# z and y in one product of 384 columns, and the gated share added from the same slot: a fused attention and adapter kernel on one core

## The chip, the cores and the metric

The kernel runs on one core of a Trainium2 chip. The core has five engines with queues of their own: TensorE (PE, matmuls, with weight loads shown apart as PEld), VectorE (DVE), ScalarE (ACT), GpSimd (POOL) and SyncE (SP), and 16 DMA engines. Engines wait for each other through semaphores, and each works through its own instructions in order. The metric is the device time of one execution in microseconds (us), the median of several runs.

## The reference

```
qn, kn = q, k divided by their norms over the 6400 tokens
a = softmax(kn^T @ qn / tau)              # 256 x 256 for each of 4 batches
x = v @ a                                 # 25600 tokens x 256
logits = x @ w_gate                       # 8 experts; the best two are kept
w = softmax over the two kept
out = x + sum over the two: w_e * (x @ A_e) @ B_e     # A_e 256x16, B_e 16x256
```

The kernel never forms x to take the logits and the adapters' inner products: with wa = a @ [w_gate, A] (256 x 136) it has logits = v @ wa[:, 0:8] and z = v @ wa[:, 8:136]; then gz = z times the gate of its expert, and out = y + gz @ B with y = v @ a, B being all eight B_e as 128 x 256.

## The kernel before, in words

A chunk is 128 tokens; two chunks are a pair, and there are 100 pairs, 25 for each of four batches. For a batch, q and k are read first. `square` (ACT, or DVE in batch 0) squares them, `gram` (L294) sums k^T q over the 50 chunks in PSUM, and `norm` (L305 for batch 0, L311 for the others) sums the squares. `chain0` to `chain6` then turn the sums into a and wa for the batch.

A pair goes through these steps:

- `transposes` (PE, L444) turns the pair's v so that tokens can be the stationary operand; ACT (L452) or DVE (L454) copies it to SBUF as vT.
- `logits` (PE, L465), for five pairs together, and `gating`, thirteen small operations for five pairs, all but one on DVE (L489 to L534), that give the gates.
- `z_gz`: z on PE (L551, four matmuls of 128 columns), then DVE multiplies by the gates, gz (L555).
- `gz_t`: PE transposes gz (L575) into a spare part of z's bank; DVE (L581), and ACT at the end (L579), copies it out, gzT.
- `y_mm`: y on PE (L567, four matmuls of 256 columns).
- `delta`: PE adds gzT @ B onto y (L587); ACT copies the sum to the output ring `ys` (L591). Full groups leave by DMA from ACT's queue (`send`, L617), the last ones from SP's (L595).

The order is written by hand: the main loop (L678 on) goes through numbered slots, and each engine gets its instructions in the order in which the loop issues them. Slots 8 to 22, 26 to 46 and 50 to 68 also take two to four chunks of `gram` and `norm` for the next batch; the chain's steps lie in the seven slots after each of these stretches. From slot 73 on there is no gram left: this is the tail. Transposes run eight slots ahead of the pair that is gated. Where five further pairs are ready, the loop puts in an iteration of pair work alone, without transposes, gram or a new slot (`behind`); there are six of these.

In a slot the order on PE is: z of pair u; transposes of gz of the pair before, u-1 (`zq`); the first half of the slot's gram; y of the pair u-2 (`dq`); transposes of v for a later pair; the share of u-2; logits every fifth slot; the other half of the gram. A pair so takes three slots. DVE's gating operations are dealt out at a slot's end, up to a sum of estimated costs (`deal`). PSUM has eight banks: one each for gram sums and norm sums, two each for transposed v, z and y; in the tail z also uses the banks of the sums.

Loads are issued by POOL, in a fixed order, as soon as the buffer that they need is free (`load_more`); q, k and v are cast to bf16 on the way.

Of the kernel before, what the change touches and what calls it, by code (L numbers as in the profile page):

```python
# [16 lines left out]
def kernel(  # L17
# [16 lines left out]
    nc = tc.nc  # L34
# [38 lines left out]
    sq_pool = ctx.enter_context(tc.tile_pool(name="sqp", bufs=4))  # L73
    vt_pool = ctx.enter_context(tc.tile_pool(name="vtp", bufs=14))
    y_pool = ctx.enter_context(tc.tile_pool(name="yp", bufs=1))
# [3 lines left out]
    work = ctx.enter_context(tc.tile_pool(name="work", bufs=3))  # L79
    ps_acc = ctx.enter_context(tc.tile_pool(name="psacc", bufs=1, space=bass.MemoryType.PSUM))  # L80
    ps_nrm = ctx.enter_context(tc.tile_pool(name="psnrm", bufs=1, space=bass.MemoryType.PSUM))
    ps_t = ctx.enter_context(tc.tile_pool(name="pst", bufs=2, space=bass.MemoryType.PSUM))
    ps_z = ctx.enter_context(tc.tile_pool(name="psz", bufs=2, space=bass.MemoryType.PSUM))
    ps_y = ctx.enter_context(tc.tile_pool(name="psy", bufs=2, space=bass.MemoryType.PSUM))

# [139 lines left out]

    wg_sb = const.tile([P, CC, E], BF16)
    A_sb = const.tile([P, CC, E, R], BF16)
    ball_sb = const.tile([P, C], BF16)
# [24 lines left out]
    def spread():  # L253

        ap = ps_t.tile([P, 512], FP32, tag="pt", name="A_ps")[:, 0:CC * ER].rearrange(
            "p (c d) -> p c d", c=CC)
        for cc in range(CC):
            for j in range(DL // CC):
                nc.tensor.matmul(ap[:, cc, :], sel[:, E - j:E - j + P], rows[:, j * CC + cc, :],
                                 start=(cc == 0 and j == 0),  # L260
                                 stop=(cc == CC - 1 and j == DL // CC - 1), skip_group_check=True)
        nc.scalar.copy(A_sb.rearrange("p cc e r -> p cc (e r)"), ap)

    def cast_constants():
        nc.vector.tensor_copy(wg_sb.rearrange("p cc e -> p (cc e)"), wst)
        nc.vector.tensor_copy(ball_sb, bst)
# [21 lines left out]
    def gram(b, c):  # L288
        if c == 0:
            acc[b] = ps_acc.tile([P, CC, C], FP32, tag="acc", name="acc")  # L290
        s, o = qk_piece(c)
        t = tiles["qk"][b, s]
        for ic in range(CC):
            nc.tensor.matmul(  # L294
                acc[b][:, ic, :], t[:, 1, o, ic * P:(ic + 1) * P], t[:, 0, o, :],
                start=(c == 0 and ic == 0), stop=(c == NC - 1), skip_group_check=True)
        used("qk", b, c, 1)

    def norm(b, c):
        if c == 0:  # L300
            nrm[b] = ps_nrm.tile([P, 512], FP32, tag="nrm", name="nrm")
        sq = sqs[b, c - c % 2]
        if b == 0:

            nc.tensor.matmul(nrm[b].rearrange("p (w d) -> p w d", w=2), ones_bf, sq[:, :, c % 2, :],  # L305
                             start=(c == 0), stop=(c == NC - 1))
# [52 lines left out]
    def chain3(b):  # L359
        d = st[b]  # L360
        ae = bat.tile([P, CC, C], BF16, name="ae")
# [4 lines left out]
        d["ae"], d["se"] = ae, se  # L366

# [17 lines left out]
    def chain5(b):  # L385
# [4 lines left out]
        for ic in range(CC):  # L390
            for cc in range(CC):
                nc.tensor.matmul(wa[:, ic, 0:E], aT[:, cc, ic * P:(ic + 1) * P], wg_sb[:, cc, :],
                                 start=(cc == 0 and ic == 0), stop=False, skip_group_check=True)
                nc.tensor.matmul(wa[:, ic, E:E + ER], aT[:, cc, ic * P:(ic + 1) * P],
                                 A_sb[:, cc, :, :].rearrange("p e r -> p (e r)"),
                                 start=False, stop=(cc == CC - 1 and ic == CC - 1),
                                 skip_group_check=True)
        wa_sb = bat.tile([P, CC, E + ER], BF16, name="wa_sb")
        for ic in range(CC):
            nc.vector.tensor_scalar(out=wa_sb[:, ic, :], in0=wa[:, ic, :],  # L400
                                    scalar1=rec[:, ic:ic + 1], scalar2=None, op0=OP.mult)
        d["wa"] = wa_sb

    def chain6(b):
        d = st[b]
        a_bf = d["ae"]
        for ic in range(CC):
            nc.vector.tensor_scalar(out=a_bf[:, ic, :], in0=a_bf[:, ic, :],
                                    scalar1=d["rec"][:, ic:ic + 1], scalar2=None, op0=OP.mult)
        d["a"] = a_bf  # L410

# [18 lines left out]
    LAST = {NPT - 9: 4, NPT - 6: 6, NPT - 4: 4, NPT - 3: 2, NPT - 2: 2, NPT - 1: 2}  # L430

    def transposes(g, eng):

# [4 lines left out]
        vt = tiles["v"][b, s]  # L438
        full = ps_t.tile([P, 512], FP32, tag="pt", name="vT_ps")
        pt = full[:, 0:256].bitcast(BF16).rearrange("p (c t) -> p c t", c=CC)  # L440
# [17 lines left out]
    def logits(gr):  # L458
# [4 lines left out]
        for sc in range(n):  # L463
            for ic in range(CC):
                nc.tensor.matmul(lp[:, sc, :], pr[gr["f"] + sc // 2]["vT"][:, ic, sc % 2, :],  # L465
                                 st[b]["wa"][:, ic, 0:E],
                                 start=(sc == 0 and ic == 0), stop=(sc == n - 1 and ic == 1),
# [72 lines left out]

    def z_gz(u):
        b = u // NPAIR
        r, gr = pr[u], groups[u]

        banks = [(ps_z, "zg"), (ps_z, "zg"), (ps_acc, "acc"), (ps_nrm, "nrm")]
        pool, tag = banks[u % 4 if free_banks[0] else 0]
        zg = pool.tile([P, 512], FP32, tag=tag, name="zg")
        z = zg[:, 0:256].rearrange("p (s d) -> p s d", s=2)
        for sc in range(2):
            for ic in range(CC):  # L550
                nc.tensor.matmul(z[:, sc, :], r["vT"][:, ic, sc, :], st[b]["wa"][:, ic, E:E + ER],  # L551
                                 start=(sc == 0 and ic == 0), stop=(sc == 1 and ic == 1),
                                 skip_group_check=True)
        gz = work.tile([P, 2, ER], BF16, tag="gz", name="gz")
        nc.vector.tensor_tensor(  # L555
            out=gz.rearrange("p c (e r) -> p c e r", e=E),
            in0=z.rearrange("p c (e r) -> p c e r", e=E),
            in1=gr["gate"][:, r["w"]:r["w"] + 2, :].to_broadcast([P, 2, E, R]), op=OP.mult)
        r["gz"], r["zg"] = gz, zg

    def y_mm(u):
        b = u // NPAIR
        r = pr[u]
        y = ps_y.tile([P, 2, C], FP32, tag="y", name="y_ps")
        for sc in range(2):
            for ic in range(CC):
                nc.tensor.matmul(y[:, sc, :], r["vT"][:, ic, sc, :], st[b]["a"][:, ic, :],  # L567
                                 start=(sc == 0 and ic == 0), stop=False, skip_group_check=True)
        r["y"] = y
# [14 lines left out]
    def delta(u):  # L584
        r, gr = pr.pop(u), groups[u]
        for sc in range(2):
            nc.tensor.matmul(r["y"][:, sc, :], r["gzT"][:, sc, :], ball_sb, start=False,  # L587
                             stop=(sc == 1), skip_group_check=True)
        if "ys" not in gr:
            gr["ys"] = ring_ys[:, gr["at"], :, :]  # L590
        nc.scalar.copy(gr["ys"][:, r["w"]:r["w"] + 2, :], r["y"])  # L591
        if u in LAST:
# [50 lines left out]
    for f, _ in CHAIN:  # L643
        for g, eng in between.get(f, []):
            transposes(g, eng)
        f(0)
# [31 lines left out]
    while nz < NPT or zq is not None or dq is not None:  # L678
# [14 lines left out]
        if nz < min(slot, NPT) and groups[nz]["ready"]:  # L693
            u = nz
            nz += 1
            z_gz(u)
        if zq is not None:
            gz_t(zq, "act" if slot >= NPT else "dve")
        gram_part(items[:h])
        if dq is not None:  # L700
            y_mm(dq)
        if slot < NPT and not behind:
            transposes(slot, "dve" if items or f is chain3 else "act")
        if dq is not None:
            delta(dq)
        dq, zq = zq, u
        send(max(0, DEFER - max(0, slot - FLUSH) // 3))
# [54 lines left out]
```

## Time and profile before

| | |
|---|---|
| median of 3 runs | 254.23 us (254.2 to 254.32) |
| the profiled execution | 254.42 us, its span 252.6 us |
| PE busy | 219.8 us, 87% |
| weight loads (PEld) | 191.7 us, 76% |
| DVE busy | 154.6 us, 61% |
| ACT busy | 177.5 us, 70% |
| granted PE clock, mean | 0.97 |
| HBM | 78.91 MB read, 26.21 MB written |

The profile is one execution. A row of a timeline has start, length, engine, line, operation, what it writes and reads, and how often; in brackets, the idle time of its engine before it and what ended that. A PE record is longer than the time for which it holds PE, since matmuls are pipelined; the distance between starts gives the latter. A row of stretches has the busy time of each engine in a stretch, the granted clock, the DMA engines' share and what they moved. A row of groups has a line's instructions together: busy time, mean ns of one, idle time before it and what ended it.

### The profile page before, as it was taken

The page shows a single profiled execution, that of the slowest core. Times are in us where ns is not written, and L with a number is a line of the kernel's source. Part 1 is how long each engine was busy: PE and PEld are TensorE (multiplying, and loading weights), DVE is VectorE, ACT ScalarE, POOL GpSimd, SP SyncE. Part 2 cuts the span into 40 slices and gives each one's busy share as a digit, 9 for nine tenths or more (in the row PEclk, how much of TensorE's full clock was granted, in tenths as well). Part 3 has the DMA queues.
Part 4 walks back from the last instruction along what each step waited for, and adds up shares of the span by engine and source line. Part 5 has one row for each costly group of instructions (what it writes and reads, how often), then busy time and mean ns, then how long its engine had stood idle before and what let it go on. Part 6 is the DMA issues. An engine that isn't in the chain of part 4 may idle for free.

```text
span 252.6 us, 7407 instructions
## 1 busy us (share of the span) xinstructions
PE 219.8 (87%) x3122; PEld 191.7 (76%) x3122; DVE 154.6 (61%) x581; ACT 177.5 (70%) x297; POOL 29.8 (12%) x60
## 2 busy tenths in 40 slices
PE   0478877786999999999999999999899799999990
PEld 0235554566899999889999889889798688999970
DVE  1216524655447577776776877858477677776750
ACT  2415532674698979978788798788687677887881
POOL 8210110102012101240220100000001000000000
PEclk9999999659799999999999999999999999999998
DMA  7999999999999999999999999999999999999996
GB/s 213 221 223 214 219 217 211 217 212 218 216 216 213 215 216 213 211 216 213 211 217 220 212 259 270 258 276 296 246 246 353 346 308 413 423 431 417 406 417 259
DMA packets 10577, 66.80 MB, mean 264 GB/s; under 512 B 1584, under 2 KB 1840, under 8 KB 7984
## 3 DMA queue, kind: packets, MB, share of 16 engines
q0 software_dynamic: 7088, 38.80, 74.4%
q10 hardware_dynamic: 1872, 23.59, 22.3%
q1 hardware_dynamic: 1584, 3.94, 4.3%
q8 instruction: 24, 0.39, 0.6%
q14 instruction: 9, 0.07, 0.1%
HBM read 78.91 MB, written 26.21 MB: 416 GB/s over the span
## 4 chain that ended last, share of the span: by engine, by line
PE 51%; DMA 37%; DVE 5%; ACT 3%; POOL 1%; issue 1%; DVEq 0%; POOLq 0%
DMA qk<-in_k_dram 37%; PE y_ps L567 14%; PE acc L294 8%; PE y_ps L587 6%; PE zg L551 6%; PE vT_ps L444 6%; PE zg L575 4%; PE nrm L311 3%; PE vT_ps L465 3%; DVE gz L555 1%; ACT sq L284 1%; ACT ys L591 1%; POOL qk L183 1%; DVE e L497 0%; DVE lg L489 0%
## 5 line engine op out<-in xcount | busy, mean ns | idle before, releaser
L284 ACT ACTIVATE sq<-qk 128x1024 bf16<-128x1024 bf16 (+1 forms) x90 | 89.7, 1026 | 22.6 <-DMA qk<-in_k_dram 16.9
L294 PE MATMUL acc<-qk 128*128 128x256 bf16 x400 | 73.5, 285 | 18.5 <-DMA qk<-in_k_dram 12.1
L591 ACT COPY ys<-y_ps 128x512 f32<-128x512 f32 x100 | 58.7, 588 | 20.7 <-PE y_ps L587 18.7
L567 PE MATMUL y_ps<-ae,vT 128*128 128x256 bf16 x400 | 60.5, 274 | 0.3 <-ACT ys L591 0.3
L294 PEld LDWEIGHTS <-qk 128*128 128x128 bf16 x400 | 34.0, 101 | 28.2 <-DMA qk<-in_k_dram 14.0
L555 DVE TENSOR_TENSOR gz<-zg,gate 128x256 bf16<-128x256 f32 x100 | 41.6, 416 | 14.8 <-PE zg L551 13.0
L311 PEld LDWEIGHTS <-sq 128*128 128x128 bf16 x600 | 36.3, 97 | 6.3 <-ACT sq L284 2.5
L454 DVE COPY vT<-vT_ps 128x512 bf16<-128x512 bf16 x60 | 25.3, 422 | 24.5 <-PE vT_ps L444 23.3
L551 PE MATMUL zg<-wa_sb,vT 128*128 128x128 bf16 x400 | 38.7, 220 | 0.8 <-DVE gzT L581 0.8
L587 PE MATMUL y_ps<-ball_sb,gzT 128*128 128x256 bf16 x200 | 38.6, 275 | 0.0
L311 PE MATMUL nrm<-ones_bf,sq 128*128 128x1 bf16 x600 | 35.6, 164 | 1.3 <-ACT sq L284 1.2
L567 PEld LDWEIGHTS <-vT 128*128 128x128 bf16 x400 | 33.6, 97 | 3.2 <-issue 0.4
L452 ACT COPY vT<-vT_ps 128x512 bf16<-128x512 bf16 x40 | 23.5, 587 | 12.1 <-PE vT_ps L444 10.7
L444 PE MATMUL vT_ps<-ident,vt 128*128 128x128 bf16 x300 | 30.1, 226 | 1.8 <-DVE vT L454 1.5
L575 PE MATMUL zg<-ident,gz 128*128 128x128 bf16 x200 | 27.7, 221 | 1.5 <-DVE gz L555 1.1
L551 PEld LDWEIGHTS <-vT 128*128 128x128 bf16 x400 | 26.3, 97 | 2.7 <-issue 1.3
L444 PEld LDWEIGHTS <-vt 128*128 128x128 bf16 x300 | 23.3, 101 | 4.6 <-issue 2.2
L581 DVE COPY gzT<-zg 128x256 bf16<-128x256 bf16 x90 | 25.1, 279 | 0.0
L286 DVE TENSOR_TENSOR sq<-qk 128x1024 bf16<-128x1024 bf16 (+1 forms) x14 | 9.1, 653 | 21.9 <-DMA qk<-in_k_dram 13.1
L575 PEld LDWEIGHTS <-gz 128*128 128x128 bf16 x200 | 15.1, 98 | 3.1 <-DVE gz L555 2.9
L183 POOL DMA_DIRECT2D qk<-in_q_dram x16 | 8.8, 550 | 69.4 <-PE acc L294 27.6
L587 PEld LDWEIGHTS <-gzT 128*128 128x128 bf16 x200 | 16.3, 99 | 0.5
(77 smaller groups left out, 197.8 us busy)
## 6 DMA issues: line engine op xcount, KB each, us to landing
out_dram<-ys ACTq DMA_DIRECT2D x7, 1280.0 KB, 11.9
out_dram<-ys ACTq DMA_DIRECT2D x2, 3840.0 KB, 24.6
qk<-in_q_dram POOLq DMA_DIRECT2D x8, 768.0 KB, 26.5
qk<-in_k_dram POOLq DMA_DIRECT2D x8, 768.0 KB, 30.0
qk<-in_q_dram POOLq DMA_DIRECT2D x7, 832.0 KB, 24.4
qk<-in_k_dram POOLq DMA_DIRECT2D x7, 832.0 KB, 27.9
out_dram<-ys ACTq DMA_DIRECT2D x2, 2560.0 KB, 20.4
vt<-in_v_dram POOLq DMA_DIRECT2D x4, 1024.0 KB, 34.9
```

The source lines that it names most:

```text
L284: nc.scalar.activation(dst, src, ACT.Square)
L294: nc.tensor.matmul(acc[b][:, ic, :], t[:, 1, o, ic * P:(ic + 1) * P], t[:, 0, o, :], start=(c == 0 and ic == 0), stop=(c == NC - 1), skip_ ...
L311: nc.tensor.matmul(nrm[b][:, j:j + 1], sq[:, w, c % 2, ic * P:(ic + 1) * P], ones_bf[:, 0:1], start=(c == 0 and j == 0), stop=(c == NC - 1 ...
L444: nc.tensor.matmul(pt[:, ic, sc * P:(sc + 1) * P], vt[:, o + sc, ic * P:(ic + 1) * P], ident, is_transpose=True, start=(i == 0), stop=(i = ...
L454: nc.vector.tensor_copy(dst, src)
L551: nc.tensor.matmul(z[:, sc, :], r["vT"][:, ic, sc, :], st[b]["wa"][:, ic, E:E + ER], start=(sc == 0 and ic == 0), stop=(sc == 1 and ic == ...
L555: nc.vector.tensor_tensor(out=gz.rearrange("p c (e r) -> p c e r", e=E), in0=z.rearrange("p c (e r) -> p c e r", e=E), in1=gr["gate"][:, r ...
L567: nc.tensor.matmul(y[:, sc, :], r["vT"][:, ic, sc, :], st[b]["a"][:, ic, :], start=(sc == 0 and ic == 0), stop=False, skip_group_check=True)
L575: nc.tensor.matmul(gt[:, sc, :], r["gz"][:, sc, :], ident, is_transpose=True, start=(sc == 0), stop=(sc == 1))
L581: nc.vector.tensor_copy(gzT, gt)
L587: nc.tensor.matmul(r["y"][:, sc, :], r["gzT"][:, sc, :], ball_sb, start=False, stop=(sc == 1), skip_group_check=True)
L591: nc.scalar.copy(gr["ys"][:, r["w"]:r["w"] + 2, :], r["y"])
```

## The change

z and y of a pair have the same stationary operand, vT. The scaled a and wa now lie beside each other in one tile `ya`, so that one matmul of 384 columns gives z and y of a chunk. A pair's product takes two banks, a chunk in each; two pairs are in PSUM (in the tail three, the third in the banks of the sums, which are now one tile of two banks). The gated z is transposed into the last quarter of a bank of transposed v, that of the slot before where there is one. The slot's order is new. Outside the tail: share of the pair before; product; first half of the gram; transposes of gz of the same pair; transposes of v; logits; second half of the gram (without a gram, v's transposes come before gz's). In the tail: share of pair u-2, transposes of gz of pair u-1, transposes of v, product of pair u, logits. w_gate and A lie in one tile as well (`ga_sb`), so that `chain5` has one matmul where it had two. vT has 12 buffers where it had 14.

```
+    ga_sb = const.tile([P, CC, E + ER], BF16)
...
+            both = ps_sum.tile([P, 2, 512], FP32, tag="sum", name="acc")
+            acc[b] = both[:, 0, :].rearrange("p (c d) -> p c d", c=CC)
+            nrm[b] = both[:, 1, :]
...
+        ya = bat.tile([P, CC, E + ER + C], BF16, name="ya")
+        ae = ya[:, :, E + ER:]
...
+    def bank():
+
+        if pts[0] is None:
+            pts[0] = ps_t.tile([P, 512], FP32, tag="pt", name="vT_ps")
+        return pts[0]
...
-    def z_gz(u):
+    def yz_gz(u):
...
+        if free_banks[0] and u % 3 == 0:
+            t = ps_sum.tile([P, 2, 512], FP32, tag="sum", name="yz")
+        else:
+            t = ps_yz.tile([P, 2, 512], FP32, tag="yz", name="yz")
         for sc in range(2):
             for ic in range(CC):
+                nc.tensor.matmul(t[:, sc, 0:ER + C], r["vT"][:, ic, sc, :], st[b]["ya"][:, ic, E:],
+                                 start=(ic == 0), stop=False, skip_group_check=True)
...
-        gt = r["zg"][:, 256:384].bitcast(BF16).rearrange("p (s d) -> p s d", s=2)
+        gt = (bank() if pts[1] is None else pts[1])[:, 512 - ER:].bitcast(BF16).rearrange("p (s d) -> p s d", s=2)
...
+        pts[:] = [None, pts[0]]
         load_more()
+        if dq is not None:
+            delta(dq)
...
-            z_gz(u)
-        if zq is not None:
-            gz_t(zq, "act" if slot >= NPT else "dve")
-        gram_part(items[:h])
-        if dq is not None:
-            y_mm(dq)
-        if slot < NPT and not behind:
-            transposes(slot, "dve" if items or f is chain3 else "act")
-        if dq is not None:
-            delta(dq)
-        dq, zq = zq, u
+        if free_banks[0]:
+            if zq is not None:
+                gz_t(zq, "act" if slot >= NPT else "dve")
+            if slot < NPT and not behind:
+                transposes(slot, "act")
+            if u is not None:
+                yz_gz(u)
+            dq, zq = zq, u
+        else:
+            if u is not None:
+                yz_gz(u)
+            gram_part(items[:h])
+            if u is not None and items:
+                gz_t(u, "dve")
+            if not behind:
+                transposes(slot, "dve" if items or f is chain3 else "act")
+            if u is not None and not items:
+                gz_t(u, "dve")
+            dq = u
```

More of the change, by code (lines that the diff above doesn't have):

```diff
@@ L438, in transposes @@
         vt = tiles["v"][b, s]
-        full = ps_t.tile([P, 512], FP32, tag="pt", name="vT_ps")
+        full = bank()
         pt = full[:, 0:256].bitcast(BF16).rearrange("p (c t) -> p c t", c=CC)
@@ L556, in z_gz @@
             out=gz.rearrange("p c (e r) -> p c e r", e=E),
-            in0=z.rearrange("p c (e r) -> p c e r", e=E),
+            in0=t[:, :, 0:ER].rearrange("p c (e r) -> p c e r", e=E),
             in1=gr["gate"][:, r["w"]:r["w"] + 2, :].to_broadcast([P, 2, E, R]), op=OP.mult)
[L559 to L569, printed above, removed]
+        r["gz"], r["yz"] = gz, t
     def gz_t(u, eng):
         r = pr[u]
-        gt = r["zg"][:, 256:384].bitcast(BF16).rearrange("p (s d) -> p s d", s=2)
+        gt = (bank() if pts[1] is None else pts[1])[:, 512 - ER:].bitcast(BF16).rearrange("p (s d) -> p s d", s=2)
         for sc in range(2):
@@ L585, in delta @@
         r, gr = pr.pop(u), groups[u]
+        y = r["yz"][:, :, ER:ER + C]
         for sc in range(2):
-            nc.tensor.matmul(r["y"][:, sc, :], r["gzT"][:, sc, :], ball_sb, start=False,
-                             stop=(sc == 1), skip_group_check=True)
+            nc.tensor.matmul(y[:, sc, :], r["gzT"][:, sc, :], ball_sb, start=False,
+                             stop=True, skip_group_check=True)
         if "ys" not in gr:
             gr["ys"] = ring_ys[:, gr["at"], :, :]
-        nc.scalar.copy(gr["ys"][:, r["w"]:r["w"] + 2, :], r["y"])
+        nc.scalar.copy(gr["ys"][:, r["w"]:r["w"] + 2, :], y)
         if u in LAST:
```

43 lines of the change are left out of this document (12 added, 31 removed).

## The prediction

> **What bounds the kernel now.** I read the page's busy table, its DMA slices and the chain that ended last, then the stretches, to see in which stage that chain lies.
>
> ```profile
> span 252.6 us, 7407 instructions
> ...
> PE 219.8 (87%) x3122; PEld 191.7 (76%) x3122; DVE 154.6 (61%) x581; ACT 177.5 (70%) x297; POOL 29.8 (12%) x60
> ...
> DMA  7999999999999999999999999999999999999996
> ...
> PE 51%; DMA 37%; DVE 5%; ACT 3%; POOL 1%; issue 1%; DVEq 0%; POOLq 0%
> ```
>
> ```profile
> 62.00:80.00 18.00, 18.00 (x268) 16.34 (x266) 10.13 (x37) 14.10 (x21) 2.65 (x5) 0.91 1.04 216
> ...
> 120.00:142.00 22.00, 22.00 (x369) 20.66 (x367) 16.14 (x62) 17.67 (x28) 3.67 (x7) 1.00 1.05 215
> 142.00:160.00 18.00, 17.81 (x287) 16.06 (x285) 13.85 (x55) 16.74 (x29) 1.63 (x4) 1.00 1.04 251
> 160.00:179.00 19.00, 17.69 (x279) 16.12 (x278) 12.62 (x47) 14.32 (x22) 0.00 (x0) 1.00 1.03 282
> ...
> 190.00:200.00 10.00, 8.80 (x137) 7.80 (x135) 7.08 (x31) 7.75 (x19) 0.72 (x2) 1.00 1.01 356
> ...
> 249.00:253.00 4.00, 0.00 (x0) 0.00 (x0) 0.00 (x0) 0.00 (x0) 0.00 (x0) 0.76 0.35 136
> ```
>
> Columns: stretch, its length, busy time of PE, PE's weight loads, DVE, ACT and POOL, then granted clock, DMA share, GB/s. Two resources are full at once. The DMA engines work through the span; only the last stretch has slack, 65% of its 3.6 us, some 2 us. PE idles for long only before 62 us; afterwards it is nearly gapless, 1.31 us short in the 160 to 179 stretch, 1.2 us in 190 to 200. So the kernel cannot get more than about 2 us faster, and anything that makes PE wait after 62 us goes into the end.
>
> **What PE pays per pair.** One tail slot, on PE, in order; the distance from one start to the next is what the instruction holds PE for (its own record is longer by the pipeline's drain):
>
> ```profile
> 221.00 0.39 PE L551 MATMUL zg<-wa_sb,vT 128*128 128x128 bf16 x4
> 221.22 0.28 PE L575 MATMUL zg<-ident,gz 128*128 128x128 bf16 x2
> 221.33 0.60 PE L567 MATMUL y_ps<-ae,vT 128*128 128x256 bf16 x4
> 221.77 0.39 PE L444 MATMUL vT_ps<-ident,qk 128*128 128x128 bf16 x4
> 221.99 0.38 PE L587 MATMUL y_ps<-ball_sb,gzT 128*128 128x256 bf16 x2
> 222.21 0.65 PE L465 MATMUL vT_ps<-wa_sb,vT 128*128 128x8 bf16 x20
> 222.71 0.38 PE L551 MATMUL zg<-wa_sb,vT 128*128 128x128 bf16 x4
> ```
>
> z 0.22, transposes of gated z 0.11, y 0.44, transposes of v 0.22, share 0.22: 1.21 us a pair, and 0.50 for the logits every five pairs. A matmul of 128 columns holds PE 55 ns, one of 256 columns 110 ns. Wider ones, from the start of the kernel:
>
> ```profile
> 20.28 0.60 PE L305 MATMUL nrm<-sq,ones_bf 128*128 128x512 bf16 x2
> 20.71 0.60 PE L294 MATMUL acc<-qk 128*128 128x256 bf16 x4
> ```
>
> 0.43 us for two of 512 columns, 215 ns each. The price is columns, with nothing fixed beside it.
>
> ```profile
> L284 ACT ACTIVATE sq<-qk 128x1024 bf16<-128x1024 bf16 (+1 forms) x90 | 89.7, 1026 | 22.6 <-DMA qk<-in_k_dram 16.9
> ...
> L591 ACT COPY ys<-y_ps 128x512 f32<-128x512 f32 x100 | 58.7, 588 | 20.7 <-PE y_ps L587 18.7
> ...
> L567 PEld LDWEIGHTS <-vT 128*128 128x128 bf16 x400 | 33.6, 97 | 3.2 <-issue 0.4
> ```
>
> **The change, part by part.**
>
> *The product.* 400 z matmuls and 400 y matmuls become 400 of 384 columns: between 110 and 215 ns, on the line through 55, 110 and 215 some 163 ns, so 0.65 us a pair where z and y held 0.66. Gain: 1 us over 100 pairs. Bounds: no gain by columns; at most the 97 ns of a weight load for each of 400 loads, 39 us, had weight loads set the pace; the three widths say they don't. [...]
>
> *The order in a slot.* Before, a gated z was transposed one slot after its z, its share added two after. Each wait had a slot over it. The very end shows the bare chain, since nothing is left to lie over it:
>
> ```profile
> 243.65 0.61 PE L551 MATMUL zg<-wa_sb,vT 128*128 128x128 bf16 x8
> ...
> 244.07 0.76 DVE L555 TENSOR_TENSOR gz<-zg,gate 128x256 bf16<-128x256 f32 x2 [0.16 <-PE zg L551]
> ...
> 244.55 0.62 PE L575 MATMUL zg<-ident,gz 128*128 128x128 bf16 x4 [0.29 <-DVE gz L555]
> ...
> 244.92 0.70 ACT L579 COPY gzT<-zg 128x256 bf16<-128x256 bf16 x2 [0.49 <-PE zg L575]
> ```
>
> PE is through with the first z at 243.87 (four of 55 ns), DVE starts the gating 0.20 later, PE the transposes 0.48 after that: 0.68 us from product to transposes. From there to the copy's start 0.32 (a 0.28 record and a short handover; ACT here took 0.37), the copy 0.28 on DVE (below), 0.06 back: 0.66 to the share. These two waits are what the new order has to cover; PE executes in order, so all that stands behind a waiting transpose waits with it, the next transposes of v, and through them ACT's copies.
>
> *Tail (slots 76 on, pairs 65 to 99).* The loop issues share, transposes of gated z, transposes of v, product; the transposes belong to the product issued last. Between them stands one share, 0.22: stall 0.68 - 0.22 = 0.46, a pair 1.21 + 0.45 = 1.66 us. Where logits stand behind the product (5 slots) they cover it. Some 19 slots with transposes of v, 2 catch-up iterations and 8 after slot 100: 29 x 0.45 = 13.0; against it PE's idle in today's tail,
>
> ```profile
> 200.00:246.00 46.00, 44.01 (x620) 39.90 (x617) 33.31 (x147) 35.27 (x76) 0.00 (x0) 1.00 1.00 399
> ```
>
> 2 us, waits for gates, of which the slower loop hides about 1.5. **+11.5.**
>
> *Gram slots.* Now product, half of the gram, gated transposes, transposes of v, other half; share at the head of the next slot.
>
> ```profile
> 118.42 0.24 PE zg L551 x4
> ...
> 128.81 0.24 PE zg L551 x4
> ```
>
> ```profile
> 118.61 0.38 PE L294 MATMUL acc<-qk 128*128 128x256 bf16 x2
> ...
> 118.94 0.38 PE L294 MATMUL acc<-qk 128*128 128x256 bf16 x2
> ```
>
> ```profile
> L454 DVE COPY vT<-vT_ps 128x512 bf16<-128x512 bf16 x60 | 25.3, 422 | 24.5 <-PE vT_ps L444 23.3
> L581 DVE COPY gzT<-zg 128x256 bf16<-128x256 bf16 x90 | 25.1, 279 | 0.0
> ...
> L497 DVE TENSOR_TENSOR e<-lg,m 128x80 f32<-128x80 f32 (+2 forms) x21 | 5.0, 238 | 0.7
> ```
>
> Five slots from one z to the z five pairs on (the chain's rows): 10.39 us for 12 chunks of 0.33. After, count from the start of a gating: transposes of gated z at 0.48 (the first half, 0.33 to 0.66, lies within 0.68 and hides nothing more), to 0.59, v's 0.81, one chunk 1.14, share 1.36, product 2.01, handover 2.21. So a slot of 2 chunks costs 2.2 as one of 3 does, where today it is 1.87 and 2.2. DVE in the same slot: gating, copy of gated z 0.80 to 1.08, copy of v to 1.50, three gating operations of 0.27 with gaps to 2.3. In the fifth slot the logits write the bank that gated z was just transposed into and wait for its copy: 1.14 + 0.48, in all 3.0. Five slots: 3.0 + 4 x 2.25 = 12.0, +1.6 (13 chunks: +1.3). For 40 slots of batches 2 and 3, 8 x 1.45 = 11.6; the 10 slots of batch 1 after 62 us have 3 or 4 chunks, +1.5. **+13.**
>
> *Slots without a gram* (23 to 25, 47 to 49, 69 to 72) cover the first wait with v's transposes, 0.22, and the second with nothing: 0.46 + 0.55 = 1.0 on 1.21; nine pairs, less where logits or the chain's own matmuls fill in: **+8**. Catch-up iterations (4 before the tail) cover neither: 0.68 + 0.55 = 1.2 each, **+5**.
>
> *The rest.* Product tiles of two banks: three pairs in flight in the tail, two before, each next user a slot after the ACT copy that frees it: ACT has 0.59 for the copy and 1.03 for each square (one or two a slot) in a slot of 2.2 us, so it keeps up on average: nothing, and up to 2 x 1.03 + 0.59 - 2.2 = 0.45 in a slot of two squares. Gram and norm sums in one tile: the next batch waits for the chain's last read, which DVE has done before the gating that PE waits for anyway: nothing. Chain step 5 issues 16 matmuls of 8 columns fewer, at 25 ns (0.50 for 20 logits) 0.4 us: nothing. A transposed v is done with after the product, two slots sooner than after y, so 12 buffers do what 14 did. Loads keep their order on POOL; a buffer comes free later with PE, but a queue of 26 us (below) lies over the delay. ACT and SP issue outputs where they did.
>
> ```profile
> qk<-in_q_dram POOLq DMA_DIRECT2D x8, 768.0 KB, 26.5
> ```
>
> The last column is the median time from issue to landing. Output leaves later; the DMA backlog at the end shrinks, up to the 2 us above: -1.
>
> **Sum** against this execution, 254.42 (span 252.6): 11.5 + 13 + 8 + 5 = 37.5, less 1 for the product, 1 for the end and 2.5 for idle PE after 62 us that the new stalls swallow: +33, 287. Against the median of 254.23: 286.
>
> **Rivals.**
>
> *The middle is paced by loads.* The chain has one DMA piece there:
>
> ```profile
> 142.02 36.87 DMA qk<-in_k_dram
> ```
>
> If stalls before 179 us vanished in it, only slots 69 to 72 (+3.5), some five gram slots (+1.5) and the tail (+11.5) count: 254 + 16.5 - 2 = 268. Against: PE is 96% busy in those 37 us (17.81 of 18, 17.69 of 19), so there are 1.5 us to vanish in.
>
> *The clock drops.*
>
> ```profile
> 43.54 0.38 PE L444 MATMUL vT_ps<-ident,vt 128*128 128x128 bf16 x4 [1.46 <-DVE vT L454]
> ```
>
> ```profile
> 42.00:46.00 4.00, 1.73 (x16) 1.13 (x14) 3.19 (x10) 2.14 (x6) 0.53 (x1) 1.00 1.05 218
> 46.00:50.00 4.00, 3.22 (x37) 2.37 (x37) 2.45 (x9) 2.31 (x7) 0.53 (x1) 0.54 1.07 224
> ```
>
> After a stretch with PE 43% busy it ran at 0.54. New slots hold PE 72% in the tail and 55% without a gram. If each of the three gram-free stretches is followed by 4 us at half clock, +2 each, and a few such windows fall in the tail: +8, 294. Against: no clock loss at the 88% of 190 to 200. [...]
>
> *Faster: weight loads set PE's pace.* PE's loads are busy 76% of the span; if a fused product saved the whole 97 ns of its dropped load, 39 us, it would outweigh +33 and DMA would end it: 254.2 - 2 = 252. It decides from 0.33 us saved per pair; by the three widths it is 0.01.
>
> **How the numbers follow.** Stalls as summed 0.72, clock 0.12, middle hidden 0.11, faster 0.04, no change 0.01. A measurement tells 0.2% from no change, so faster 0.04, same 0.01, slower 0.95. The sum's own range is 275 to 296 (the waits at 0.55 or 0.75 rather than 0.68, DVE's gating dealt unluckily); with the two slow rivals 267 to 298.
>
> **What would show it.** On PE after the change: product 0.65 a pair; an idle of about 0.46 us before the transposes of gated z in the tail, released by DVE's gating, 1.66 from product to product; gram slots of 2 and 3 chunks at the same 2.2 to 2.3; DMA share well under 1 in the last 60 us; PE's idle after 62 us near 35 us. Wrong if products take clearly less than 0.65, if the order on PE leaves more than a share between product and transposes, or if PE's waits are for loads.

## The result and the profile after

The changed kernel takes 292.66 us (median of 6 runs, 291.12 to 294.2) against 254.23 us (6 runs, 254.1 to 254.4) for the kernel before: a ratio of 1.151, 95% interval 1.148 to 1.155. It is slower by 38 us; 286 was predicted, with a range of 267 to 298. The profiled execution took 292.55 us, its span is 290.7.

The page of the changed kernel, the lines that answer to those shown of before:

```profile
span 290.7 us, 6651 instructions
...
PE 238.5 (82%) x2706; PEld 170.0 (58%) x2706; DVE 163.4 (56%) x581; ACT 179.7 (62%) x297; POOL 29.3 (10%) x60
...
PEclk9988997599999999999999599999999999999999
DMA  7999999999999999999999999924199998844444
...
PE 65%; DVE 16%; DMA 10%; ACT 3%; issue 3%; POOL 1%; DVEq 0%; ACTq 0%; POOLq 0%
...
L551 PE MATMUL yz<-ya,vT 128*128 128x384 bf16 x400 | 83.0, 331 | 0.0
...
L564 PE MATMUL vT_ps<-ident,gz 128*128 128x128 bf16 x200 | 28.7, 226 | 17.6 <-DVE gz L554 16.3
```

There are 416 matmuls fewer on PE and PE is busy for a smaller share (82%, 87% before). The weight loads fell from 76% to 58% of the span while the time rose by 15%. In the chain that ended last, DMA went from 37% to 10% and DVE rose from 5% to 16%: what ends late now is PE with DVE between its steps. The DMA engines, full to the end before, are partly idle from 189 us on, full again from 211 to 240 us, and idle for more than half of the time in the last 36 us. Two stretches:

```profile
180.00:200.00 20.00, 18.08 (x235) 14.15 (x233) 12.49 (x46) 14.60 (x22) 0.00 (x0) 1.00 0.54 147
260.00:270.00 10.00, 8.97 (x104) 5.62 (x101) 6.60 (x26) 6.39 (x13) 0.00 (x0) 1.00 0.32 133
```

(Columns as in the prediction: PE, PEld, DVE, ACT, POOL, then granted clock, DMA share, GB/s.) The DMA share is 0.54 and 0.32 there, and the clock is 1.00. After 62 us the profile puts no wait of PE down to a DMA. So neither loads nor clock hold the kernel in these stretches.

What PE waits for over the whole span, in us in total, times, longest:

```profile
PE vT_ps L564 <- DVE gz L554: 16.3, 54, 0.7
PE acc L293 <- DMA qk<-in_k_dram: 7.3, 3, 3.4
...
PE yz L577 <- DVE gzT L570: 4.5, 11, 0.5
PE vT_ps L465 <- DVE gzT L570: 2.5, 12, 0.5
PE acc L350 <- ACT tk L343: 2.3, 2, 1.2
```

The first, third and fourth rows are the two chains that the prediction named: the transposes of gated z (L564) wait for the gating, and the share (L577) or the logits (L465) for the copy of what was transposed. A wait is counted here from the end of PE's record, which is longer than the time for which it holds PE (0.81 us against 0.65 for a product), so the sum of these rows, 23 us, is less than the loss. By the records PE is idle for 30 us between 62 and 287 us (near 35 predicted), and for 5 us between 62 and 246 us before.

Where the time went, by the start of the product (of z before) of each pair; columns: us from the first pair's start to the second's.

| pairs | what lies there | before | after | difference |
|---|---|---|---|---|
| 2 to 15 | gram of batch 1 | 29.71 | 31.83 | +2.1 |
| 15 to 18 | no gram, chain | 4.70 | 7.77 | +3.1 |
| 18 to 38 | rest of the chain, gram of batch 2 | 42.60 | 50.77 | +8.2 |
| 38 to 42 | no gram, chain | 8.31 | 14.12 | +5.8 |
| 42 to 61 | rest of the chain, gram of batch 3 | 41.84 | 46.31 | +4.5 |
| 61 to 65 | no gram, chain | 10.78 | 13.83 | +3.1 |
| 65 to 99 | tail | 43.88 | 57.52 | +13.6 |

Together +40.3; pair 2 starts 0.4 later, and from the start of the last product it is 6.10 us to the end instead of 8.76, -2.7. That is the +38.1 of the spans, but for rounding.

One pair of the tail in the timeline, up to the next pair's product (start, length, then engine and line):

```profile
258.46 0.81 PE L551 MATMUL yz<-ya,vT 128*128 128x384 bf16 x4
...
259.11 0.38 PE L577 MATMUL yz<-ball_sb,gzT 128*128 128x256 bf16 x2
259.32 0.42 DVE L554 TENSOR_TENSOR gz<-yz,gate 128x256 bf16<-128x256 f32 x1 [0.51 <-PE yz L551]
...
259.80 0.28 PE L564 MATMUL vT_ps<-ident,gz 128*128 128x128 bf16 x2 [0.30 <-DVE gz L554]
...
259.92 0.39 PE L444 MATMUL vT_ps<-ident,qk 128*128 128x128 bf16 x4
...
260.14 0.81 PE L551 MATMUL yz<-ya,vT 128*128 128x384 bf16 x4
```

Product 0.65 (258.46 to 259.11), share 0.22 (two of 110 ns), then PE stands until 259.80: 0.69 from the end of the product to the transposes, as the prediction had it (0.68). DVE starts 0.21 after the product, needs 0.42, and PE follows 0.06 later. The pair takes 1.68 where 1.66 was predicted and 1.21 stood before.

And a gram slot with two chunks:

```profile
131.11 0.81 PE L551 MATMUL yz<-ya,vT 128*128 128x384 bf16 x4
131.76 0.38 PE L293 MATMUL acc<-qk 128*128 128x256 bf16 x2
...
131.96 0.42 DVE L554 TENSOR_TENSOR gz<-yz,gate 128x256 bf16<-128x256 f32 x1
...
132.44 0.29 PE L564 MATMUL vT_ps<-ident,gz 128*128 128x128 bf16 x2 [0.22 <-DVE gz L554]
...
133.34 0.81 PE L551 MATMUL yz<-ya,vT 128*128 128x384 bf16 x4
```

One chunk of the gram covers part of the wait, the rest follows, and the slot takes 2.23 (2.2 predicted).

In the chain after batch 2's gram there is a wait that the prediction had set at nothing. First the timeline of PE, then the stretches around it:

```profile
159.12 0.70 PE L350 MATMUL acc<-dg,ones_f 128*128 128x256 f32 x2 [1.19 <-ACT tk L343]
159.65 1.27 PE L551 MATMUL yz<-ya,vT 128*128 128x384 bf16 x4
```

```profile
158.00:160.00 2.00, 0.89 (x4) 0.59 (x5) 0.76 (x4) 1.54 (x4) 0.00 (x0) 0.97 0.92 193
160.00:162.00 2.00, 1.74 (x9) 0.78 (x7) 1.09 (x4) 0.59 (x1) 0.35 (x1) 0.50 1.03 254
```

The matmul that spreads the norms over the partitions (L350) writes the norms' half of the shared tile, and now waits for ACT's reading (L343) of the gram's half. PE is busy for 45% of these 2 us, and then the granted clock is 0.50; the next product has a record of 1.27 instead of 0.81.

### The profile page after: what moved, and what is told of

Read it like the earlier page. It is cut to its first block, busy times and chain, and to the rows that moved or that the text cites. A ratio compares the mean times of both kernels' runs of the same rounds, so it can differ in the third digit from the quotient of the medians.

```text
span 290.7 us, 6651 instructions
## 1 busy us (share of the span) xinstructions
PE 238.5 (82%) x2706; PEld 170.0 (58%) x2706; DVE 163.4 (56%) x581; ACT 179.7 (62%) x297; POOL 29.3 (10%) x60
## 4 chain that ended last, share of the span: by engine, by line
PE 65%; DVE 16%; DMA 10%; ACT 3%; issue 3%; POOL 1%; DVEq 0%; ACTq 0%; POOLq 0%
PE yz L551 22%; PE acc L293 11%; DMA qk<-in_k_dram 10%; DVE gz L554 9%; PE vT_ps L564 9%; PE yz L577 7%; PE vT_ps L444 6%; PE vT_ps L465 4%; PE acc L308 4%; DVE gzT L570 3%; PE acc L302 1%; ACT ys L581 1%; POOL qk L181 1%; DVE ya L394 1%; PE acc L350 1%
## 5 line engine op out<-in xcount | busy, mean ns | idle before, releaser
L581 ACT COPY ys<-yz 128x512 f32<-128x512 f32 x100 | 58.2, 582 | 54.6 <-PE yz L577 47.0
L293 PE MATMUL acc<-qk 128*128 128x256 bf16 x400 | 74.6, 288 | 13.8 <-DMA qk<-in_k_dram 7.3
L551 PE MATMUL yz<-ya,vT 128*128 128x384 bf16 x400 | 83.0, 331 | 0.0
L554 DVE TENSOR_TENSOR gz<-yz,gate 128x256 bf16<-128x256 f32 x100 | 42.3, 423 | 45.5 <-PE yz L551 43.6
L551 PEld LDWEIGHTS <-vT 128*128 128x128 bf16 x400 | 37.9, 98 | 15.5 <-issue 0.9
L577 PE MATMUL yz<-ball_sb,gzT 128*128 128x256 bf16 x200 | 38.8, 276 | 5.9 <-DVE gzT L570 4.5
L564 PE MATMUL vT_ps<-ident,gz 128*128 128x128 bf16 x200 | 28.7, 226 | 17.6 <-DVE gz L554 16.3
L570 DVE COPY gzT<-vT_ps 128x256 bf16<-128x256 bf16 x90 | 26.2, 291 | 27.5 <-PE vT_ps L564 25.5
L308 PE MATMUL acc<-ones_bf,sq 128*128 128x1 bf16 x600 | 35.6, 164 | 1.1 <-ACT sq L281 1.1
L452 ACT COPY vT<-vT_ps 128x512 bf16<-128x512 bf16 x40 | 23.5, 588 | 11.9 <-PE vT_ps L444 11.9
L564 PEld LDWEIGHTS <-gz 128*128 128x128 bf16 x200 | 11.6, 98 | 32.5 <-DVE gz L554 31.6
L283 DVE TENSOR_TENSOR sq<-qk 128x1024 bf16<-128x1024 bf16 (+1 forms) x14 | 9.3, 664 | 21.8 <-DMA qk<-in_k_dram 10.8
L577 PEld LDWEIGHTS <-gzT 128*128 128x128 bf16 x200 | 12.9, 97 | 14.1 <-DVE gzT L570 8.4
L302 PE MATMUL acc<-sq,ones_bf 128*128 128x512 bf16 x50 | 16.7, 426 | 0.0
L465 PEld LDWEIGHTS <-vT 128*128 128x128 bf16 x400 | 13.2, 97 | 5.2 <-issue 4.5
```

The lines of the kernel that those rows point to most:

```text
L293: nc.tensor.matmul(acc[b][:, ic, :], t[:, 1, o, ic * P:(ic + 1) * P], t[:, 0, o, :], start=(c == 0 and ic == 0), stop=(c == NC - 1), skip_ ...
L308: nc.tensor.matmul(nrm[b][:, j:j + 1], sq[:, w, c % 2, ic * P:(ic + 1) * P], ones_bf[:, 0:1], start=(c == 0 and j == 0), stop=(c == NC - 1 ...
L551: nc.tensor.matmul(t[:, sc, 0:ER + C], r["vT"][:, ic, sc, :], st[b]["ya"][:, ic, E:], start=(ic == 0), stop=False, skip_group_check=True)
L554: nc.vector.tensor_tensor(out=gz.rearrange("p c (e r) -> p c e r", e=E), in0=t[:, :, 0:ER].rearrange("p c (e r) -> p c e r", e=E), in1=gr[ ...
L564: nc.tensor.matmul(gt[:, sc, :], r["gz"][:, sc, :], ident, is_transpose=True, start=(sc == 0), stop=(sc == 1))
L570: nc.vector.tensor_copy(gzT, gt)
```

## The experiments

Theory: PE's order is what costs. Transposes of a gated z stand too close behind its product, and the share too close behind the transposes; the work between them has to come from other pairs. Rivals: the wider matmul or the number of weight loads sets the pace; loads pace the middle, so that shorter slots there bring nothing; the tiles in PSUM (sums in one tile, products of two banks) are what holds PE.

**e1_split: the product as z and y again, in the same order and the same banks.** 400 matmuls and weight loads more.

```diff
-    nc.tensor.matmul(t[:, sc, 0:ER + C], r["vT"][:, ic, sc, :], st[b]["ya"][:, ic, E:],
+    nc.tensor.matmul(t[:, sc, 0:ER], r["vT"][:, ic, sc, :], st[b]["ya"][:, ic, E:E + ER],
                      start=(ic == 0), stop=False, skip_group_check=True)
+    nc.tensor.matmul(t[:, sc, ER:ER + C], r["vT"][:, ic, sc, :], st[b]["ya"][:, ic, E + ER:],
+                     start=False, stop=False, skip_group_check=True)
```

> The changed kernel with its order and its banks, but the product of 384 columns taken apart again into 128 and 256 columns, 400 matmuls and weight loads more. Exposed waits (my theory): columns are the price, so 0.66 us a pair instead of 0.65: 293 to 295. Weight loads set PE's pace: 400 times up to 97 ns more, 310 to 330.

Measured: 293.36 us, ratio to before 1.156 (1.151 to 1.161), beside 1.151 (1.148 to 1.155) for the changed kernel. The intervals overlap: by the medians 400 more matmuls and weight loads cost 0.7 us, where 400 times 97 ns would be 39 us. In stretches where the clock is full in both traces (pairs 2 to 15, 18 to 38, 42 to 61) e1_split takes 0.37 us more over 52 pairs, 0.007 a pair, which is 0.7 over 100. The pace is not set by weight loads, and what the change is named for, one product of 384 columns, is worth next to nothing. That leaves the order and the banks. (The fewer buffers of vT were not tested alone. In the changed kernel's profile the copies into them wait for their own transposes: 11.9 of ACT's 11.9 us and 3.5 of DVE's 3.7.)

**e2_tail: other work between the two steps in the tail.** Half of the product (chunk 0), transposes of the gated z of pair u-1, the other half, transposes of v, share of u-1.

```diff
+            if sc == 0 and between is not None:
+                between()
...
-            if zq is not None:
-                gz_t(zq, "act" if slot >= NPT else "dve")
+            def turn(w=zq):
+                if w is not None:
+                    gz_t(w, "act" if slot >= NPT else "dve")
+            if u is not None:
+                yz_gz(u, turn)
...
                 transposes(slot, "act")
-            if u is not None:
-                yz_gz(u)
-            dq, zq = zq, u
+            if zq is not None:
+                delta(zq)
+            dq, zq = None, u
```

> The changed kernel with another order in the tail alone: the transposes of gated z of pair u-1 stand between the two chunks of the product of pair u, the share of u-1 after the transposes of v. Product and all else are as they were. Exposed waits: a tail pair goes from 1.68 back to about 1.25, 35 pairs, 278 to 282. If the tail were slow for ACT, DVE or banks and not for that wait: 289 or more.

Measured: 287.4 us, 1.131 (1.129 to 1.134): 5.3 us gained where 11 to 15 were expected, between the two expectations. The tail (pairs 65 to 99) went from 57.5 to 53.1 us. PE's timeline shows why it wasn't more; the second fence is DVE's and ACT's:

```profile
250.24 0.49 PE L551 MATMUL yz<-ya,vT 128*128 128x384 bf16 x2
250.78 0.27 PE L566 MATMUL vT_ps<-ident,gz 128*128 128x128 bf16 x2
```

```profile
249.92 0.42 DVE L556 TENSOR_TENSOR gz<-yz,gate 128x256 bf16<-128x256 f32 x1
...
250.15 0.58 ACT L452 COPY vT<-vT_ps 128x512 bf16<-128x512 bf16 x1 [0.42 <-PE vT_ps L444]
```

The half product is through at 250.57 (two at 162 ns), and the gating of the pair before was done at 250.34; yet the transposes start at 250.78. They write the last quarter of the bank of transposed v of the slot before, and ACT is copying that bank until 250.73. One wait was replaced by another, on the bank that the change put gated z into.

**e3_gram: the order outside the tail.** Product of u, share of u-1, gram, transposes of v, and the transposes of u's gated z at the slot's end.

```diff
-        if dq is not None:
+        if dq is not None and free_banks[0]:
             delta(dq)
...
                 yz_gz(u)
+            if dq is not None:
+                delta(dq)
             gram_part(items[:h])
-            if u is not None and items:
-                gz_t(u, "dve")
...
         gram_part(items[h:])
+        if u is not None and not free_banks[0]:
+            gz_t(u, "dve")
```

> The changed kernel with another order outside the tail alone: product of u, share of u-1, gram, transposes of v, then the transposes of gated z of u at the slot's end. Exposed waits: a gram slot of 2 chunks goes from 2.23 to about 1.85, the slots without a gram from 2.25 to about 1.5, so 20 to 25 us less, 268 to 273. The middle is paced by loads: 288 or more, since the stalls before the last load were hidden.

Measured: 281.26 us, 1.107 (1.101 to 1.112), 11.4 us faster than the changed kernel and between the two expectations: 20 to 25 were expected. The rival that loads pace the middle is refuted: pair 64 starts at 208.06 instead of 221.07, 13.0 earlier, and the gain reaches the end. Some slots with two chunks now take 1.84, about what their columns need, others 2.28; the stretch 21 to 38 takes 37.36 (41.87 in the changed kernel, 34.21 before). A part of what is left shows in the waits and in one of the slots; the last two rows are ACT's:

```profile
PE yz L551 <- ACT ys L581: 5.0, 9, 1.2
```

```profile
129.27 0.81 PE L551 MATMUL yz<-ya,vT 128*128 128x384 bf16 x4 [0.28 <-ACT ys L581]
```

```profile
127.70 1.04 ACT L281 ACTIVATE sq<-qk 128x1024 bf16<-128x1024 bf16 x1
128.65 0.56 ACT L581 COPY ys<-yz 128x512 f32<-128x512 f32 x1
```

The product waits for ACT's copy that empties the banks of the pair two before, and that copy stands behind a square. Two pairs in PSUM are too few where ACT also has squares of 1.03 us to make. In the changed kernel no product waits for such a copy; the wait was hidden behind the wait for the gating, and came out when that went.

**e5_sums: gram and norm sums in tiles of their own again**, which leaves the tail two product tiles where it had three.

```diff
-            both = ps_sum.tile([P, 2, 512], FP32, tag="sum", name="acc")
-            acc[b] = both[:, 0, :].rearrange("p (c d) -> p c d", c=CC)
-            nrm[b] = both[:, 1, :]
+            acc[b] = ps_sum.tile([P, CC, C], FP32, tag="acc", name="acc")
+            nrm[b] = ps_sum.tile([P, 512], FP32, tag="nrm", name="nrm")
...
-        if free_banks[0] and u % 3 == 0:
-            t = ps_sum.tile([P, 2, 512], FP32, tag="sum", name="yz")
-        else:
+        if True:
             t = ps_yz.tile([P, 2, 512], FP32, tag="yz", name="yz")
```

> The changed kernel with gram sums and norm sums in a tile each, as before the change, and two product tiles throughout (the tail's third is gone). If the shared tile makes the chain's broadcast matmul wait for ACT's copy of the gram sums, 2.3 us of PE's waits go and with them the dip of the clock behind the longest (3 us), against at most 1.7 in the tail for the third tile: 286 to 290. If the shared tile costs nothing: 292 to 295.

Measured: 299.32 us, 1.178 (1.173 to 1.184), a miss. Pairs 38 to 42 took 11.68 instead of 14.12, but the tail went from 57.5 to 66.9 us:

```profile
260.46 0.81 PE L548 MATMUL yz<-ya,vT 128*128 128x384 bf16 x4 [0.55 <-ACT ys L578]
```

With two tiles the product waits for ACT's copy of the pair two before. By the traces the third pair in PSUM is worth 9.3 us over 34 pairs, 0.27 a pair. Some of that is clock: e5_sums had 3.41 us at half clock from 288.85, and the steps from pair 97 to 99, which lie there, took 0.85 us longer than the changed kernel's.

**e9_sep: the same, with a third product in the two tiles of the sums**, a chunk in each; that pair is gated and copied in two halves.

```diff
         if free_banks[0] and u % 3 == 0:
-            t = ps_sum.tile([P, 2, 512], FP32, tag="sum", name="yz")
+            ts = [ps_sum.tile([P, 512], FP32, tag=g, name="yz") for g in ("acc", "nrm")]
...
+            for sc in range(2):
+                nc.vector.tensor_tensor(out=gz[:, sc:sc + 1, :]..., in0=ts[sc][:, None, 0:ER]..., ...)
```

> The changed kernel with gram sums and norm sums in a tile each; the tail's third product lies in these two, so it is gated and copied in two halves. Only the shared tile is undone: pairs 38 to 42 take 11.7 us instead of 14.1, as in e5, all else unchanged, the halves hidden off PE's path: 289 to 291. If e5's 2.4 us there came from elsewhere: 292 or more.

Measured: 289.87 us, 1.141 (1.139 to 1.143), as expected; pairs 38 to 42 took 11.68. But only a part of these 2.4 us is the tile, so that the number was met is partly luck. The e2_tail kernel and the changed one have the same instructions up to pair 64, and in e2_tail's trace the same wait of 1.19 us ends at 160.07 without a drop of the clock:

```profile
160.07 0.70 PE L350 MATMUL acc<-dg,ones_f 128*128 128x256 f32 x2 [1.19 <-ACT tk L343]
160.61 0.81 PE L551 MATMUL yz<-ya,vT 128*128 128x384 bf16 x4
```

```profile
160.00:162.00 2.00, 1.62 (x11) 1.04 (x12) 1.08 (x3) 0.81 (x3) 0.06 (x1) 1.00 1.03 212
```

e1_split has the same wait, and there the clock does drop, to 0.50 for 3.41 us; its pairs 38 to 42 take 13.27:

```profile
159.07 1.01 PE L350 MATMUL acc<-dg,ones_f 128*128 128x256 f32 x2 [1.19 <-ACT tk L343]
```

In e2_tail and in e6_tail_order (below) pairs 38 to 42 take 12.21. So 1.9 of the 2.4 us are the half clock of the changed kernel's profiled execution, and 0.5 are the tile: in e9_sep the wait is still there, for another reason, and shorter.

```profile
PE vT_ps L573 <- DVE gz L563: 12.8, 41, 0.7
...
PE nrm L349 <- DVE dg L338: 1.3, 2, 0.7
```

The second row is what remains of it (2.3 us in two places before the split, 1.3 after). The first is a gain that was not expected: 41 waits for the gating instead of 54. A pair that is gated in halves can have its first half gated while the second chunk's product runs, which would explain it; the tail took 55.8 instead of 57.5.

**e6_tail_order: a tail that avoids the bank of the last slot's v.** Share of u-2, transposes of v, the first matmul of the product, transposes of gated z of u-1, the other three.

```diff
+                if sc == 0 and ic == 0 and between is not None:
+                    between()
...
-            if zq is not None:
-                gz_t(zq, "act" if slot >= NPT else "dve")
...
                 transposes(slot, "act")
             if u is not None:
-                yz_gz(u)
+                yz_gz(u, turn)
...
             dq, zq = zq, u
```

> The changed kernel with a third order in the tail: share of u-2, transposes of v, first matmul of the product of u, transposes of gated z of u-1, the other three matmuls. The transposes of gated z, which write the bank that holds the transposed v of the slot before, now also come 0.8 us after that v, so ACT's copy of it has ended. If the order e2 was held at 1.5 us a pair by that copy: 1.3 to 1.4 a pair, 281 to 285. If DVE or ACT fills the tail at 1.5: 286 to 288, as e2.

Measured: 288.38 us, 1.133 (1.128 to 1.139), no better than e2_tail within the intervals, and just above the range that was expected if DVE or ACT filled the tail. The trace doesn't show either full: from 252 to 270 us DVE is busy for 13.8 of 18 us and ACT for 12.5. The tail takes 53.1 us instead of 57.5, as in e2_tail, but with 3.41 us at half clock at its start, from 228.23. From pair 68 on, where the clock is full in all three, it takes 47.98 us, against 48.99 in e2_tail and 52.49 in the changed kernel. Its pairs take 1.34 where nothing else stands:

```profile
249.82 0.33 PE L551 MATMUL yz<-ya,vT 128*128 128x384 bf16 x1
...
249.98 0.28 PE L566 MATMUL vT_ps<-ident,gz 128*128 128x128 bf16 x2
...
250.09 0.65 PE L551 MATMUL yz<-ya,vT 128*128 128x384 bf16 x3
...
250.71 0.39 PE L579 MATMUL yz<-ball_sb,gzT 128*128 128x256 bf16 x2
...
251.16 0.33 PE L551 MATMUL yz<-ya,vT 128*128 128x384 bf16 x1
```

The transposes start 0.16 after the first matmul, without a wait. That 1.34 is still not the 1.21 of before, since the copy that the share needs is late instead (PE stands from 250.58 to 250.71). In two slots, those behind a catch-up iteration, the gated z still goes into the bank that ACT is copying v out of, and waits:

```profile
236.93 0.27 PE L566 MATMUL vT_ps<-ident,gz 128*128 128x128 bf16 x2 [0.78 <-ACT vT L452]
```

Its profiled execution also started pair 0 at 58.77 where the changed kernel's did at 56.35, with a clock of 0.50 from 56 to 60 us (0.82 there), in instructions that are the same in both. Three of its four executions had a mean clock of 0.956 to 0.959 and took 288.4 to 289.7 us; the fourth, at 0.977, took 286.0. Whether the lower clock comes with this order is not shown.

**e7_gram_squares: e3_gram with the second square of a slot issued behind the share's copy on ACT.**

```diff
-        for b, c in items:
-            if c % 2 == 0:
-                square(b, c, "act")
+        even = [(b, c) for b, c in items if c % 2 == 0]
+        for b, c in even[:1]:
+            square(b, c, "act")
...
             delta(dq)
+            for b, c in even[1:]:
+                square(b, c, "act")
```

> The order of e3 (281.3) with a slot's second square issued on ACT behind the copy of the share instead of ahead of it. If the rest of the loss in the gram slots, 0.5 us in five slots, is the product waiting for that copy to free its banks: 276 to 279. If it is something else: 280.5 to 283.

Measured: 277.92 us, 1.095 (1.092 to 1.099), in the range expected, but not as expected. The gain over e3_gram lies in four single slots, at pairs 9, 18, 41 and 54, of 0.75 to 0.95 us each (the stretch 45 to 55 took 22.09 instead of 23.03); the repeated loss in the stretch 21 to 38 stayed (37.36 in both), since the copy there stands behind the slot's first square, as in the rows above. And the DMA engines show as a limit again (share 1.01 from 170 to 192 us), in ACT's timeline:

```profile
190.49 0.59 ACT L581 COPY ys<-yz 128x512 f32<-128x512 f32 x1 [2.03 <-DMA out_dram<-ys]
```

The copy waits for an output DMA that has not yet left its place in the ring; PE waits 1.78 us for it, and the stretch 55 to 61 took 15.57 instead of 13.10 in e3_gram.

**e8_all: e6, e7 and e9 together.**

> e6, e7 and e9 in one: the fused product, two waits covered in both parts, sums apart. If the three losses are separate and add up: 292.7 - 9 - 15.5 - 2.5, so 263 to 268, still slower than before since slots without a gram keep a stall. If PE's waits only change places: 272 or more.

Measured: 272.08 us, 1.071 (1.069 to 1.073), the fastest version that keeps the product of 384 columns, and slower than the kernel before by 17.9 us. The single gains over the changed kernel were 4.3, 14.7 and 2.8, together 21.8; 20.6 came. They add up but for 1.2 us. The time is that of the other expectation (272 or more, if PE's waits only change places), but for another reason: the expectation of 263 to 268 had counted on 9 us from the order in the tail, where e6_tail_order then gave 4.3. Waits of its PE:

```profile
PE vT_ps L575 <- DVE gz L565: 3.3, 10, 0.5
PE yz L552 <- ACT ys L595: 3.0, 6, 1.6
```

The wait for the gating is 3.3 instead of 16.3 us. What still separates it from the kernel before lies in the tail (51.9 us against 43.9), in the stretches without a gram and the gram of batch 3 (43.6 against 40.3 from pair 45 to 64), and in the gram of batch 2 (37.36 against 34.21). No single wait stands out there, and the cause of the rest stays open.

## Why the prediction was right, and where it was off

- **The product: right.** 0.65 us a pair, 162 ns a matmul, on the line through 55, 110 and 215. Splitting it again (e1_split) costs 0.7 us where the step had a gain of 1. The rival that weight loads set the pace fell with that.
- **The two waits: right in size and place.** 0.69 from product to transposes against 0.68; an idle of 0.47 in a tail pair where 0.46 was said (from 259.33, the end of the share's columns, to 259.80); the pair at 1.68 against 1.66.
- **The tail: +13.6 against +11.5.** The stalls were sized right: 27 pairs took 1.68 or 1.46 us, 0.48 longer than product, transposes and share hold PE, 12.9 in all where 13.0 stood for 29. What was missed is the rest. In the two slots behind a catch-up iteration there is no bank of an earlier slot; the gated z goes into the bank of the slot's own v, whose transposes then wait for DVE's copy (row below). These pairs take 2.22 us, 1.0 more than their matmuls, where 0.45 was said. And in four slots the logits don't cover the stall fully: 1.84 us instead of the 1.70 of their matmuls. Of the old tail's idle time, 3.2 us by the distance of starts, the longest piece, 1.5 us before the product of pair 98, stayed (2.48 us from pair 97 to 98 before, 2.62 after); 1.7 went, where 1.5 was said.

```profile
235.60 0.38 PE L444 MATMUL vT_ps<-ident,qk 128*128 128x128 bf16 x4 [0.38 <-DVE gzT L570]
```

- **Gram slots and catch-up iterations: right within 1 us.** +13 and +5, less 0.65 of the product's gain and the 2.5 us of idle, is 14.9; the stretches 2 to 15, 18 to 38, 42 to 61 and from pair 64 to 65, with the later start, give 15.7. There is some luck in that: the kernel before ran at half clock from 63.36 to 66.77, in the first of these stretches, and the changed kernel did not. PE was busy throughout there (18.00 of 18 us from 62 to 80), so by an estimate that is worth 1.7 us, and without it the loss would be some 17.4. Slots of two chunks took 2.23, with logits 3.03 (137.81 to 140.84 in the trace), as said.
- **Slots without a gram: +11.5 against +8.** Two of the three stretches took 3.1 and 2.6 where 2.7 each was the term. The third took 5.8: 1.9 us of it are the half clock, 0.5 the sums in one tile.
- **"Gram and norm sums in one tile: nothing": wrong.** The step looked for who reuses the tile, the next batch, and not for the chain's own matmul that writes one half while ACT reads the other. It cost 1.0 us of waiting in two places (2.3 against 1.3), 0.5 on the path after 62 us.
- **"Product tiles of two banks: nothing": right only because something else was slower.** In the changed kernel no product waits for ACT's copy. With the gating out of the way it does (5.0 us in e3_gram), and with two tiles in the tail too (9.3 us in e5_sums). Single waits in e3_gram go up to 1.2 us. The bound of 0.45 was worked out for slots of 2.2 us; by the same working a slot of 1.84 gives 0.81, and that is too low as well.
- **The end: -2.7 against -1.** The last output lands 2.0 us after its issue (287.81 to 289.81) instead of 4.6 (247.13 to 251.72). That is all but 0.1 of the difference: the backlog was worth 2.6 us, and with a DMA share of 0.46 from 254 to 290 us nothing of it is left.
- **Loads pace the middle: refuted** by e3_gram, where the 13.0 us that its trace has won at pair 64 are still won at the end (spans of 277.7 and 290.7), and by PE's waits, none of which after 62 us is for a DMA.
- **The clock drops: true in part.** The rival put 2 us behind each of three gram-free stretches. In the changed kernel's trace one of them has a drop (6.83 us at half clock from 159.87), and it lost 1.9. In the traces that share its order there, e1_split has two (3.41 us each, from 159.32 and 227.59), e6_tail_order one (from 228.23) and e2_tail none. The traces with another order there, before included, and those with the sums in separate tiles have none there. So this order can bring the drop, and whether it comes differs from trace to trace. In the changed kernel's tail, where PE is idle in nearly every pair (busy for 47.30 us of the 55.5 from 228.5 to 284, and for 90% from 260 to 270), the clock stays at 1.00, so none of the stretches at half clock that the rival had in the tail is there.

In sum, the waits were sized well and the total came out 5 us low (by the profiled execution, 287 against 292.55): 1.9 clock, 0.5 the shared tile, 1.1 the other slots without a gram, 0.8 the gram slots, 2.5 the tail (its part of the product's gain with it), less 1.7 at the end.

## What to carry to other kernels

Fusing matmuls that share a stationary operand saved 0.7 us here, where matmuls cost by columns (55, 110, 162 and 215 ns for 128, 256, 384 and 512). Count what the fusion does to the order and to the PSUM banks, which here cost 38 us; other orders brought back 20.6 of them. In an engine that works in order, the time between a product and the step that reads its result through another engine must be filled with other pairs' work: write down that latency (here 0.7 us twice) and the columns that stand between, slot by slot, the slots without filler included. When one such wait is removed, look at once for the next reader or writer of the same bank: the first reorderings here brought back about half of what was expected, and uncovered the next wait.

## What the runs showed of the hardware that was not expected

- Two halves of one PSUM tile are not independent in this program: a matmul into one half waited 1.19 us for ACT's reading of the other; with separate tiles (e9_sep) it waited 0.59 there, for its own operand. The two halves are two banks, as the separate tiles are, so by this comparison the wait comes from how the program orders uses of one tile and not from a shared bank. Transposes into the last quarter of one bank likewise waited for a copy of another part of it (0.21 us in e2_tail, from 250.57 to 250.78, and 0.78 in a slot of e6_tail_order); whether that comes from the program or from the bank, the runs don't tell apart.
- But for the one at the very end of each trace, the stretches at half clock in all ten traces last 3.41 us or a whole multiple of it: 3.41, 6.83, 10.24 or 13.65 (10.24 and 3.41 before the change; 3.41, 10.24 and 6.83 in the changed kernel). The one from 159.87 followed 2 us with PE 45% busy, whose longest wait was 1.19 us. With the same wait e1_split had 3.41 us at half clock, and e2_tail (PE busy for 0.62 of 2 us) and e6_tail_order had none. Why the drop comes in one trace and not in another with the same wait, the runs don't show.
- The runs of the changed kernel spread over 3.1 us, those of the kernel before over 0.3 us. A drop as the one above would be a good part of that, but only one of the runs has a trace, so this isn't shown.
